# Attention and a gated two-layer product on one core: weight transfers issued by another engine, decoding moved, the last partial product reordered

## The chip, the cores and the metric

One Trainium2 chip, one of its cores. TensorE (PE) multiplies, VectorE (DVE), ScalarE (ACT) and GpSimd (POOL) work on elements, and SyncE (SP) issues transfers; ACT can issue transfers too. Each engine takes its instructions in the order in which the program lists them. The metric is the device time of one execution in microseconds (us), lower is better. The kernel before took 1116.28 us, the median of 1116.28, 1114.55 and 1116.56.

## The reference

```python
def _attn_ref(q, k, v):                    # 8 batches, 12 heads, S = 448, D = 64
    scale = 1.0 / np.sqrt(q.shape[-1])
    scores = scale * np.matmul(q, k.transpose(0, 1, 3, 2)) - np.log(S)
    attn = 1.0 / (1.0 + np.exp(-scores))
    return np.matmul(attn, v)
...
x = attn_out.transpose(0, 2, 1, 3).reshape(B * S, H * D)     # 3584 x 768
h = x @ w_in                                                 # 3584 x 2048
g = h * np.clip(h + 3.0, 0.0, 6.0) / 6.0
return g @ w_out                                             # 3584 x 768
```

`w_in` and `w_out` come as 8-byte floats and are turned into 4-byte ones on the chip.

## The kernel before

**Products.** Both large products run as a 2x2 block scheme with seven products instead of eight (P1, P5, P6, P2, P7, P3, P4 in the order of work). Each is done in three passes, from a high and a low part of both operands. A pair of batches is one step of the block scheme, so there are four pairs, n = 0 to 3.

**Stages.** The attention of four batches comes first, then the first product of pair 0, the attention of batch 4, the first product of pair 1, the attention of batches 5 and 6, the first product of pair 2, the attention of batch 7, and the first product of pair 3. The second product of all pairs ends the program. The first product of a pair is four quads (jj = 0 to 3); a quad is seven products for two row blocks, 14 units of 9 matmuls on one line, L305.

**Around one unit of the first product.** `load_w1` (L268) brings a weight tile "raw" (four buffers) from scratch memory. `split_w` makes its high part on ACT (L274) and the low part on VectorE (L275), in a tile "w". Between the products, `seed` on ACT (L313) copies the sum of P1 into the bank of P2 before P6 goes on adding to P1's bank. `keep` (L317) holds the sum of P5, `seed2` on VectorE (L321) makes the start of P3 before P7 goes on in P1's bank, and `h22` (L325) makes a last sum before P4. ACT and VectorE apply the gate (L335, L338), VectorE forms differences (L343), and SP stores the results in scratch memory "gd" (L346).

**Decoding.** `prep(which, j, ...)` decodes the 8-byte weights, w_in for which = 0 and w_out for which = 1, in eight parts j. Each part has two loads "st" (L108), two operations on ACT (L118), ten on VectorE (L123 to L133), two additions on POOL (L137) and four sums there (L146), and seven stores to scratch memory (L151), "wd1" for w_in and "wd2" for w_out. The tile of the decoded weights is "wa".

**Second product.** `load_g` (L391) and `load_w2` (L386) bring its operands "gr" and "w2", `split_2` splits them, and `unit` (L416) is nine matmuls, three passes for each of three output chunks. `keep`, `plus` and `out` (L425, L429, L443, L446) carry sums out. `open_two` closes the memory of the attention and opens that of the second product, from which the first "gr" and "w2" tiles come.

**What sets the order.** Every piece of work is put in a list with a place, `at(place, f, ...)`, a planned time in us. The list is sorted, and PE, ACT, VectorE and POOL take their instructions in that order. A transfer issued by SP is ordered by the framework's own scheduler from the same list. A transfer's end is signalled on one of eight semaphores, which all transfers of SP and ACT use in turn; a transfer is not issued before the previous one on its semaphore has landed.

The places of the first product are set by these lines (TU is the planned time of a unit, q that of a quad's half):

```python
at(place + (2 * s - 5.3) * TU, split_w1, n, jj, k)
at(place + (2 * s - 5.3) * TU - 12, load_w1, n, jj, k)
...
at(p + 1 * TU + e, seed, i)
at(p + 5 * TU + e, seed2, i)
```

Of the kernel before, what the change touches and what calls it, by code (L numbers as in the profile page):

```python
# [15 lines left out]
B, H, S, D = 8, 12, 448, 64  # L16
DM, DF = 768, 2048
P = 128
NC = S // P
NP = H // 2  # L20
HC = DM // P // 2
HF = DF // P // 2
W = HC * P
NT = B // 2
# [9 lines left out]
P1, P5, P6, P2, P7, P3, P4 = range(7)  # L34
# [5 lines left out]
TU = 9 * TM  # L40
# [3 lines left out]
def tile_kernel(ctx: ExitStack, tc: tile.TileContext, qk, vP, w8, outT):  # L44
    nc = tc.nc
# [6 lines left out]
    def at(place, f, *args):  # L52
        todo.append((place, len(todo), f, args))

    dram = ctx.enter_context(tc.tile_pool(name="dram", bufs=1, space=bass.MemoryType.DRAM))
    wd1 = [dram.tile([P, NW, 2, W], F32, name=f"wd1_{j}", tag=f"wd1_{j}") for j in range(HF // 2)]
# [33 lines left out]
    def pair_banks(name, i=None):  # L90
        if i is None:
            i = turn[0]
            turn[0] += 1
        return four["pool"].tile([P, 2, 512], F32, tag=f"sc{i % 2}", name=name)

    def bank(name, k):
        return ps.tile([P, 512], F32, tag=f"pv{k}", name=name)
# [149 lines left out]
    def t_ops(n, c, early, upper, both, late, gap):  # L247


        b11, b12, b21, b22 = ((2 * n, c), (2 * n + 1, c), (2 * n, c + HC), (2 * n + 1, c + HC))  # L250
        for (place, copy), k, q in zip(early, (P1, P2), (b11, b21)):
            at(place, put, n, k, c, q, copy)
        at(upper[0], minus, b11, b12, b11)
        at(upper[0] + gap / 2, put, n, P5, c, b11, upper[1])
        for i, part in enumerate((
            (minus, b11, b22, b11), (put, n, P6, c, b11), (minus, b12, b22, b12), (minus, b21, b21, b11), (put, n, P4, c, b21),
        )):
            at(both + gap * i, *part)
        for (place, copy), k, q in zip(late, (P7, P3), (b12, b22)):
            at(place, put, n, k, c, q, copy)  # L260
# [3 lines left out]
    ring, rawt = {}, {}  # L264

    def load_w1(n, jj, k):
        t = one.tile([P, 2, W], F32, tag="raw", name=f"raw_{n}_{jj}_{k}", bufs=4)
        nc.sync.dma_start(out=t, in_=wd1[jj][:, k])  # L268
        rawt[n, jj, k] = t

    def split_w(keys, src):
# [10 lines left out]
    passes = ((0, 0), (0, 1), (1, 0))  # L282
# [3 lines left out]
    def quads(n, jj, place):  # L286
# [62 lines left out]
        for s, k in enumerate(range(NW)):  # L349
            at(place + (2 * s - 5.3) * TU, split_w1, n, jj, k)  # L350
            at(place + (2 * s - 5.3) * TU - 12, load_w1, n, jj, k)
            for i in range(2):
                at(place + (2 * s + i) * TU, product, i, k)
# [20 lines left out]
    x2, w2, graw, two = {}, {}, {}, {}  # L374
# [28 lines left out]
    def block(n, place):  # L403
        z, sn = {}, {}

        def unit(k, u):
            if u == 0:
                if k in (P6, P7, P4):
                    z[k] = z[P1]
                else:  # L410
                    t = pair_banks(f"y_{n}_{k}", n + (k != P1))
                    z[k] = [t[:, 0], t[:, 1], bank(f"yb_{n}_{k}", 2 * (n % 2) + (k != P1))]
            w, x = ring.pop((n, k, u)), x2.pop((n, k, u))
            for e in range(HC):
                for i, (wu, xu) in enumerate(passes):
                    nc.tensor.matmul(  # L416
                        z[k][e][:, :S], w[:, wu, e * P : (e + 1) * P], x[:, xu],
                        start=u == 0 and i == 0 and k in (P1, P5, P2, P3), stop=u == HF - 1 and i == 2,
                        skip_group_check=True,
                    )  # L420

        def keep(k):
            for e in range(HC):
                t = two["b"].tile([P, S], F32, tag=f"sn{k}{e}", name=f"sn2_{n}_{k}_{e}")
                nc.scalar.mul(t, z[k][e][:, :S], sixth)  # L425
                sn[k, e] = t

        def plus(dst, k, e, s):
            nc.vector.scalar_tensor_tensor(  # L429
                out=dst, in0=z[k][e][:, :S], scalar=sixth, in1=sn[s, e], op0=ALU.mult, op1=ALU.add  # L430
            )

        def middle():
            for e in range(HC):
                t = two["b"].tile([P, S], F32, tag=f"c12{e}", name=f"c12_{n}_{e}")
                plus(t, P6, e, P5)
                sn["c12", e] = t

        def out(k, s, eh, th):
            for e in range(HC):  # L440
                o = two["b"].tile([P, S], F32, tag="o", name=f"o_{n}_{k}_{e}", bufs=4)
                if s is None:
                    nc.scalar.mul(o, z[k][e][:, :S], sixth)  # L443
                else:
                    plus(o, k, e, s)
                nc.sync.dma_start(out=outT[2 * n + th, e + eh * HC], in_=o)  # L446

        d = HF * TU
        for k in range(NW):
            at(place + k * d - 26, load_g, n, k)  # L450
            if n == 0:
                at(place + k * d - 24, load_w2, k)
            for u in range(HF):
                at(place + k * d + u * TU, unit, k, u)
                if u % 2 == 0:
                    at(place + k * d + u * TU - 6 * TU + 0.3, split_2, n, k, u)
        e = 0.3
        at(place + 1 * d + e, keep, P1)
        at(place + 2 * d + e, keep, P5)
        at(place + 3 * d + e, middle)  # L460
        at(place + 4 * d + e, out, P2, P1, 0, 0)
        at(place + 5 * d + e, out, P7, P5, 1, 1)
        at(place + 6 * d + e, out, P3, "c12", 0, 1)
        at(place + 7 * d + e, out, P4, None, 1, 0)

# [2 lines left out]
    marks, starts, taken = [], [], {}  # L470
# [28 lines left out]
    dve, act = nc.vector.tensor_copy, nc.scalar.copy  # L499
    for c in range(HC):  # L500
        for n in range(NT):
            own = [taken[2 * n + (h % 2), c + HC * (h // 2)] for h in range(4)]
            free = marks[n - 1] + HF * q if n else 0.0
            start = marks[n]
            if n == 0:
                early = ((own[0], dve), (own[2], dve))
                upper, both, gap = (max(own[1], own[0] + 1.2), dve), own[3] + 0.1, 1.4
                late = ((own[3] + 11, dve), (own[3] + 12.5, dve))
            elif n == 1:
                early = ((free - 11.6 * TU + 2.2 * c, act), (free - 0.5 + 9 * c, dve))  # L510
                upper, both, gap = (free - 9.6 * TU + 3 * c, act), free + 0.7 + 9 * c, 1.2
                late = ((start - 5 + 1.3 * c, dve), (start + 2 * TU + 1.5 * c, act))
            else:
                early = ((free - 11.6 * TU + 2.2 * c, act), (free - 5.6 * TU + 2.2 * c, act))
                upper, both, gap = (own[1] + 0.1, dve), own[3] + 0.1, 1.2 if n < 3 or c < 2 else 0.1
                if n == 2:
                    late = ((start - 30 + 10 * c, dve), (start - 25 + 10 * c, dve))
                else:
                    late = ((start + 4 * TU + 1.5 * c, act), (start + 6 * TU + 1.5 * c, act))
            t_ops(n, c, early, upper, both, late, gap)  # L520
    for j in range(HF):
        prep(0, j, (8, 26, 44, 74, 92, 110, 128, 146)[j], 9)
    for j, place in enumerate((
        marks[0] + 40, marks[1] + 18, marks[1] + 50, starts[2] + 26, starts[2] + 45, marks[2] + 14, marks[2] + 42, marks[2] + 68
    )):
        prep(1, j, place, 12)
    at(marks[3] + 6, open_two)
    at(now + 5.5, close_one)
    first = now
    at(now - 0.01, open_four, "psy")  # L530
    for n in range(NT):
        block(n, now)
        now += NW * HF * TU
# [52 lines left out]
```

## Time and profile before

| what | us |
|---|---|
| median of three runs | 1116.28 |
| the profiled execution's own time | 1117.07 |
| its span in the trace | 1115.2 |
| first attention, A0 | 3.74 to 136.34 |
| first product, pair 0, Z0 | 136.34 to 244.06 |
| attention of batch 4, A1 | 244.06 to 276.87 |
| first product, pair 1, Z1 | 276.87 to 383.24 |
| attention of batches 5 and 6, A2 | 383.24 to 449.63 |
| first product, pair 2, Z2 | 449.63 to 564.70 |
| attention of batch 7, A3 | 564.70 to 597.51 |
| first product, pair 3, Z3 | 597.51 to 703.28 |
| second product, Y | 703.28 to 1111.12 |

The stages are cut at the first matmul of each, from the timeline of TensorE, in microseconds from the start of the span. The span is that of the hardware's record of one execution; 1.87 us of the execution's own time lie outside it. The names A0 to Y are used below. "Idle before" in a timeline row stands in brackets at its end, with the engine and line that ended the idle time.

### The profile page before, as it was taken

How to read it: one execution, taken by the hardware profiler on the slowest of the kernel's cores; microseconds unless marked ns; L12 is line 12 of the kernel's file. 1: busy time of each engine (PE TensorE's matmuls, PEld its weight loads, DVE VectorE, ACT ScalarE, POOL GpSimd, SP SyncE). 2: the span in 40 equal slices, each digit the busy share in tenths (PEclk: the TensorE clock that was granted, in tenths of full speed). 3: DMA queues.
4: the chain of work that ended last, by engine and by line, in shares of the span. 5: the costliest groups of instructions: out<-in, count | busy, mean ns of one | idle time of the engine just before them, and what ended most of it. 6: DMA issues, size and time to landing. Idle time of an engine off the chain costs nothing.

```text
span 1115.2 us, 17907 instructions
## 1 busy us (share of the span) xinstructions
PE 1087.1 (97%) x6720; PEld 880.5 (79%) x6720; DVE 816.8 (73%) x1101; ACT 622.2 (56%) x841; POOL 149.1 (13%) x102
## 2 busy tenths in 40 slices
PE   8999998999999999999899999999999999999998
PEld 3447697974998743898756889999999999999997
DVE  4898799997699869799958577766655655665663
ACT  7878845457554678544467354554554455445542
POOL 1524533200033003233300000000000000000000
PEclk9999999999999999999899999999999999999999
DMA  7997998965598746899743984674533553454341
GB/s 248 294 327 231 332 336 277 338 243 169 167 318 294 278 135 211 299 309 316 243 163 99 379 301 162 263 332 157 199 132 133 182 182 132 134 173 175 110 143 60
DMA packets 95271, 250.23 MB, mean 224 GB/s; under 512 B 10576, under 2 KB 66256, under 8 KB 90704
## 3 DMA queue, kind: packets, MB, share of 16 engines
q1 hardware_dynamic: 95040, 249.01, 64.9%
q8 instruction: 53, 0.87, 0.3%
q14 instruction: 34, 0.28, 0.1%
q10 hardware_dynamic: 144, 0.07, 0.0%
HBM read 164.63 MB, written 84.41 MB: 223 GB/s over the span
## 4 chain that ended last, share of the span: by engine, by line
PE 73%; DVE 10%; DMA 8%; issue 5%; POOL 2%; ACT 2%; SPq 0%; ACTq 0%; DVEq 0%; POOLq 0%
PE y L416 24%; PE z L305 20%; PE yb L416 12%; PE sc L198 7%; PE pv L224 7%; DMA raw<-wd 2%; DVE w L275 2%; DMA gr<-gd 2%; POOL ws L146 1%; PE sc L193 1%; DVE t L343 1%; DMA st<-wi 1%; PE pv L218 1%; DVE g L338 1%; POOL wa L137 1%
## 5 line engine op out<-in xcount | busy, mean ns | idle before, releaser
L305 PE MATMUL z<-x,w 128*128 128x448 f32 x2016 | 420.5, 371 | 14.8 <-DVE z L321 12.8
L305 PEld LDWEIGHTS z<-x,w 128*128 128x128 f32 x2016 | 383.7, 191 | 52.9 <-issue 11.4
L416 PE MATMUL y<-x,w 128*128 128x448 f32 x1344 | 307.9, 364 | 0.0
L416 PEld LDWEIGHTS y<-x,w 128*128 128x128 f32 x1344 | 252.0, 187 | 19.9
L275 DVE TENSOR_TENSOR w<-w,w 128x768 fp32r<-128x768 f32 x112 | 107.3, 958 | 147.4 <-ACT w L274 146.3
L204 ACT ACTIVATE a<-sc,bias_s 128x896 f32<-128x896 f32 x168 | 168.4, 1009 | 52.4 <-PE sc L198 37.1
L274 ACT CAST w<-w 128x768 fp32r<-128x768 f32 x112 | 93.8, 838 | 184.6 <-PE yb L416 180.9
L416 PE MATMUL yb<-x,w 128*128 128x448 f32 x672 | 171.9, 364 | 0.0
L275 DVE TENSOR_TENSOR w<-raw,w 128x768 fp32r<-128x768 f32 x112 | 124.8, 1116 | 43.9 <-ACT w L274 40.2
L198 PE MATMUL sc<-qk 64*64 64x448 f32 x1152 | 149.5, 544 | 5.5 <-DMA qk<-qk 3.7
L224 PE MATMUL pv<-a,v 64*64 64x448 f32 x1152 | 149.6, 537 | 3.5 <-DVE xr L233 1.3
L416 PEld LDWEIGHTS yb<-x,w 128*128 128x128 f32 x672 | 126.0, 187 | 9.9
L399 DVE TENSOR_TENSOR x<-gr,x 128x896 fp32r<-128x896 f32 x112 | 121.6, 1086 | 6.5 <-ACT x L398 6.5
L137 POOL TENSOR_TENSOR wa<-wa,st 128x768 f32<-128x768 f32 x32 | 64.6, 2017 | 403.2 <-DVE st L133 328.7
L274 ACT CAST w<-raw 128x768 fp32r<-128x768 f32 x112 | 93.2, 832 | 38.3 <-PE z L305 17.0
L398 ACT CAST x<-gr 128x896 fp32r<-128x896 f32 x112 | 104.9, 937 | 6.5 <-DMA gr<-gd 6.5
L198 PEld LDWEIGHTS sc<-qk 64*64 64x64 f32 x1152 | 53.5, 134 | 66.0 <-issue 43.4
L224 PEld LDWEIGHTS pv<-a,v 64*64 64x64 f32 x1152 | 54.3, 133 | 61.7 <-issue 47.2
L335 ACT ACTIVATE g<-z,bias 128x448 f32<-128x448 f32 x96 | 59.8, 633 | 75.9 <-PE z L305 43.0
L335 ACT ACTIVATE g<-snh,bias 128x448 f32<-128x448 f32 x32 | 21.5, 671 | 78.1 <-DVE snh L325 75.1
L338 DVE SCALAR_TENSOR_TENSOR g<-g,z 128x448 f32<-128x448 f32 x96 | 58.4, 613 | 6.6 <-ACT g L335 6.6
L241 DVE TENSOR_TENSOR x<-xr,x 128x448 fp32r<-128x448 f32 x84 | 56.8, 678 | 8.5 <-ACT x L240 6.4
(43 smaller groups left out, 679.0 us busy)
## 6 DMA issues: line engine op xcount, KB each, us to landing
gr<-gd SPq DMA_DIRECT2D x28, 1792.0 KB, 8.2
raw<-wd SPq DMA_DIRECT2D x112, 384.0 KB, 4.8
gd<-t SPq DMA_DIRECT2D x128, 224.0 KB, 4.0
gd<-g SPq DMA_DIRECT2D x96, 224.0 KB, 3.9
qk<-qk SPq DMA_DIRECT2D x47, 448.0 KB, 5.7
st<-wi SPq DMA_DIRECT2D x16, 768.0 KB, 5.5
wd<-ws SPq DMA_DIRECT2D x64, 192.0 KB, 5.2
st<-wo SPq DMA_DIRECT2D x16, 768.0 KB, 5.6
```

The costliest lines, as they stand in the source:

```text
L137: nc.gpsimd.tensor_tensor(out=a, in0=a, in1=e, op=ALU.add)
L198: nc.tensor.matmul(sc[halves[h], j, :S], k[halves[j], ks], q[halves[j]], start=True, stop=True)
L204: nc.scalar.activation(a, sc[:, :, :S], AF.Sigmoid, bias=bias_s, scale=scale)
L224: nc.tensor.matmul(pv[b, hp][h][halves[j], :S], v[halves[h], j * NC + c], a[halves[h], j], start=c == 0 and not (second and shared), stop= ...
L274: nc.scalar.copy(h, src)
L275: nc.vector.tensor_tensor(out=l, in0=src, in1=h.bitcast(F32), op=ALU.subtract)
L305: nc.tensor.matmul(z[i, k][:, :S], w[:, wu, c * P : (c + 1) * P], X[n, k, c][:, xu], start=m == 0 and k in (P1, P5), stop=m == 3 * HC - 1, ...
L335: nc.scalar.activation(new(i, o), src(i, o), AF.Relu, bias=bias_3, scale=1.0)
L338: nc.vector.scalar_tensor_tensor(out=g[i, o], in0=g[i, o], scalar=6.0, in1=src(i, o), op0=ALU.min, op1=ALU.mult)
L398: nc.scalar.copy(x[:, 0], src)
L399: nc.vector.tensor_tensor(out=x[:, 1], in0=src, in1=x[:, 0].bitcast(F32), op=ALU.subtract)
L416: nc.tensor.matmul(z[k][e][:, :S], w[:, wu, e * P : (e + 1) * P], x[:, xu], start=u == 0 and i == 0 and k in (P1, P5, P2, P3), stop=u == H ...
```

## The change

It has four parts. The weight loads of the first product are issued by ACT instead of SP. `open_two` is placed 24 us later in the plan. The places of the decoding are moved: w_in's parts earlier, w_out's first part later, three instead of two of w_out's parts in the attention of batches 5 and 6, and two instead of three in the first product of pair 2; with it, the casts of pair 2's last operands go from VectorE in the attention to ACT at the start of the first product. The last product of the last pair, P4, runs as 24 matmuls for one output chunk after another, and each chunk is copied out when it is done.

```diff
     def load_w1(n, jj, k):
         t = one.tile([P, 2, W], F32, tag="raw", name=f"raw_{n}_{jj}_{k}", bufs=4)
-        nc.sync.dma_start(out=t, in_=wd1[jj][:, k])
+        nc.scalar.dma_start(out=t, in_=wd1[jj][:, k])
...
+        def column(k, e):
+            if e == 0:
+                z[k] = z[P1]
+            for u in range(HF):
+                w, x = ring[n, k, u], x2[n, k, u]
+                for i, (wu, xu) in enumerate(passes):
+                    nc.tensor.matmul(
+                        z[k][e][:, :S], w[:, wu, e * P : (e + 1) * P], x[:, xu],
+                        start=False, stop=u == HF - 1 and i == 2, skip_group_check=True,
+                    )
...
-        def out(k, s, eh, th):
-            for e in range(HC):
+        def out(k, s, eh, th, es=range(HC)):
+            for e in es:
...
             for u in range(HF):
-                at(place + k * d + u * TU, unit, k, u)
+                if (n, k) != (NT - 1, P4):
+                    at(place + k * d + u * TU, unit, k, u)
                 if u % 2 == 0:
-                    at(place + k * d + u * TU - 6 * TU + 0.3, split_2, n, k, u)
+                    at(place + k * d + u * TU - 6 * TU + 0.3 - (u == HF - 2), split_2, n, k, u)
...
-        at(place + 7 * d + e, out, P4, None, 1, 0)
+        if n < NT - 1:
+            at(place + 7 * d + e, out, P4, None, 1, 0)
+        else:
+            for h in range(HC):
+                at(place + (6 + h / HC) * d + 0.01, column, P4, h)
+                at(place + (6 + (h + 1) / HC) * d + e, out, P4, None, 1, 0, (h,))
...
-                if n == 2:
-                    late = ((start - 30 + 10 * c, dve), (start - 25 + 10 * c, dve))
-                else:
-                    late = ((start + 4 * TU + 1.5 * c, act), (start + 6 * TU + 1.5 * c, act))
+                late = ((start + 4 * TU + 1.5 * c, act), (start + 6 * TU + 1.5 * c, act))
...
-        prep(0, j, (8, 26, 44, 74, 92, 110, 128, 146)[j], 9)
+        prep(0, j, (7, 22, 38, 70, 87, 104, 121, 138)[j], 9)
...
-        marks[0] + 40, marks[1] + 18, marks[1] + 50, starts[2] + 26, starts[2] + 45, marks[2] + 14, marks[2] + 42, marks[2] + 68
+        marks[0] + 50, marks[1] + 18, marks[1] + 50, starts[2] + 2, starts[2] + 19, starts[2] + 43, marks[2] + 22, marks[2] + 56
...
-    at(marks[3] + 6, open_two)
+    at(marks[3] + 30, open_two)
```

On VectorE, in the first product of pair 2, the rows ahead of quad 3's first seed2 (L321) were these before. In a name such as w_2_6_4 stand the pair, the row block and the product; wa_1_7 and st_1_7_1 are the last decoded part of w_out.

```order
L343 TENSOR_TENSOR t4_2_2_1_5461<-g21_2_2_1_5449,t2_2_2_1_5429 128x448
L123 TENSOR_SCALAR wa_1_7_5324<-wa_1_7_5324 128x768
L125 TENSOR_SCALAR wa_1_7_5324<-wa_1_7_5324 128x768
L241 TENSOR_TENSOR x_3_0_0_5491<-xr_6_0_4386,x_3_0_0_5491 128x448
L275 TENSOR_TENSOR w_2_6_4_5494<-raw_2_3_4_5365,w_2_6_4_5494 128x768
L127 SCALAR_TENSOR_TENSOR wa_1_7_5324<-st_1_7_1_5363,wa_1_7_5324 128x768
L241 TENSOR_TENSOR x_3_0_1_5510<-xr_6_1_4513,x_3_0_1_5510 128x448
L131 TENSOR_SCALAR st_1_7_1_5363<-wa_1_7_5324 128x768
L133 SCALAR_TENSOR_TENSOR st_1_7_1_5363<-st_1_7_1_5363 128x768
L275 TENSOR_TENSOR w_2_6_5_5526<-raw_2_3_5_5405,w_2_6_5_5526 128x768
L241 TENSOR_TENSOR x_3_0_2_5529<-xr_6_2_4629,x_3_0_2_5529 128x448
L321 TENSOR_TENSOR z_2_3_5_0_5541<-z_2_3_0_0_5439,sne_2_3_0_5508 128x448
```

The same stretch of VectorE now:

```order
L343 TENSOR_TENSOR t4_2_2_1_5473<-g21_2_2_1_5456,t2_2_2_1_5436 128x448
L241 TENSOR_TENSOR x_3_0_0_5503<-xr_6_0_4415,x_3_0_0_5503 128x448
L275 TENSOR_TENSOR w_2_6_4_5506<-raw_2_3_4_5372,w_2_6_4_5506 128x768
L241 TENSOR_TENSOR x_3_0_1_5521<-xr_6_1_4538,x_3_0_1_5521 128x448
L275 TENSOR_TENSOR w_2_6_5_5539<-raw_2_3_5_5412,w_2_6_5_5539 128x768
L241 TENSOR_TENSOR x_3_0_2_5542<-xr_6_2_4643,x_3_0_2_5542 128x448
L321 TENSOR_TENSOR z_2_3_5_0_5554<-z_2_3_0_0_5446,sne_2_3_0_5519 128x448
```

The five operations of decoding that stood there (L123 to L133) are gone from the stretch, and the other rows keep their order.

Counted over the whole order of VectorE, the decoding operations between one quad's second seed2 and the next quad's first are these. Before quad 1 of pair 0 there were 9 of part 7 (a tenth came between the two seed2 of quad 0) and are now 5. Before quads 1, 2 and 3 of pair 2 there were 10, 10 and 10, and are now 6, 7 and 5 (with one more between the two seed2 of quad 1 and one between those of quad 2). In the attention of batches 5 and 6 there were 20 and are now 30. Around pair 1 nothing moves.

On ACT, in the first product of pair 3, the rows from the end of quad 0's gates to the seeds of quad 1 (L313) were these before:

```order
L335 ACTIVATE g12_3_0_1_6265<-z_3_0_5_1_6161,bias_3_107 128x448
L274 CAST w_3_2_2_6273<-raw_3_1_2_6163 128x768
L335 ACTIVATE g21_3_0_0_6288<-z_3_0_0_0_6041,bias_3_107 128x448
L335 ACTIVATE g21_3_0_1_6310<-z_3_0_0_1_6065,bias_3_107 128x448
L274 CAST w_3_2_3_6317<-raw_3_1_3_6197 128x768
L313 COPY z_3_1_3_0_6333<-z_3_1_0_0_6300 128x448
L313 COPY z_3_1_3_1_6347<-z_3_1_0_1_6323 128x448
```

The same stretch of ACT now, with the semaphores that a row waits for (DMAHW0 to 7 are those of transfers):

```order
L335 ACTIVATE g12_3_0_1_6261<-z_3_0_5_1_6157,bias_3_107 128x448 [waits PE_49]
L268 DMA raw_3_1_5_6263<-wd1_1_58 128x768 [waits DMAHW3_49,DVE_49]
L274 CAST w_3_2_2_6269<-raw_3_1_2_6159 128x768
L335 ACTIVATE g21_3_0_0_6284<-z_3_0_0_0_6041,bias_3_107 128x448 [waits PE_49]
L335 ACTIVATE g21_3_0_1_6306<-z_3_0_0_1_6065,bias_3_107 128x448 [waits DMAHW4_49,DVE_49,PE_49]
L268 DMA raw_3_1_6_6308<-wd1_1_58 128x768 [waits DMAHW2_49,Activation_49]
L274 CAST w_3_2_3_6313<-raw_3_1_3_6193 128x768 [waits DMAHW0_49]
L313 COPY z_3_1_3_0_6329<-z_3_1_0_0_6296 128x448 [waits PE_49]
L313 COPY z_3_1_3_1_6343<-z_3_1_0_1_6319 128x448 [waits PE_49]
```

The two loads, which stood on SP before, now stand on ACT ahead of the cast and the seeds.

On SP, at the same place in pair 3, the rows now are these. They start at the store of quad 0's first gate; "gr" and "w2" are the first operands of the second product.

```order
L346 DMA gd_3_0_89<-g11_3_0_0_6176 128x448 [waits DMAHW1_49,DVE_49]
L391 DMA gr_0_0_6780<-gd_0_0_68 128x3584 [waits DMAHW4_49,DMAHW3_49,DMAHW6_49,DMAHW2_49,PE_49]
L386 DMA w2_0_6807<-wd2_0_61 128x3072 [waits DMAHW3_49,Activation_49]
L346 DMA gd_3_0_89<-g11_3_0_1_6191 128x448 [waits DMAHW4_49,DVE_49]
L391 DMA gr_0_1_6898<-gd_0_1_69 128x3584 [waits DMAHW5_49]
L386 DMA w2_1_6921<-wd2_1_62 128x3072 [waits DMAHW6_49,Activation_49]
L346 DMA gd_3_5_94<-g22_3_0_0_6212 128x448 [waits DMAHW0_49,DVE_49]
L346 DMA gd_3_5_94<-g22_3_0_1_6228 128x448 [waits DMAHW1_49,DVE_49]
L346 DMA gd_3_1_90<-t1_3_0_0_6247 128x448 [waits DMAHW2_49,DVE_49]
```

The operands' transfers keep their place behind the first store, as before; the two weight loads that stood among these rows are gone. The holder of DMAHW3 ahead of raw_3_1_5 is the transfer of w2_0, and the holder of DMAHW2 ahead of raw_3_1_6 is the store of t1_3_0_0.

## The prediction

> **What bounds the kernel now.** I read the summary first, then the stages, then the pauses of TensorE.
>
> ```profile
> span 1115.2 us, 17907 instructions
> PE 1087.1 (97%) x6720; PEld 880.5 (79%) x6720; DVE 816.8 (73%) x1101; ACT 622.2 (56%) x841; POOL 149.1 (13%) x102
> ```
>
> TensorE is busy 97% of the span, and the change leaves every matmul in place. So time can only come from or go into its pauses, the slow-clock stretches behind them, and the two ends. I cut the span at the matmuls into the stages named above. The columns are: stretch, length, then busy time (and instructions) of PE, weight loads, DVE, ACT and POOL, the granted clock, the DMA share and GB/s.
>
> ```profile
> 3.74:136.34 132.60, 130.02 (x1344) 67.78 (x1344) 105.20 (x144) 104.91 (x123) 52.43 (x36) 1.00 0.86 290
> 136.34:244.06 107.72, 104.68 (x509) 95.67 (x505) 99.02 (x137) 53.15 (x84) 29.88 (x18) 0.98 0.87 302
> 276.87:383.24 106.37, 104.15 (x509) 95.78 (x505) 89.19 (x129) 53.37 (x86) 18.68 (x12) 0.98 0.78 260
> 449.63:564.70 115.07, 108.36 (x508) 97.86 (x505) 103.22 (x139) 53.64 (x85) 37.36 (x23) 0.96 0.84 284
> 597.51:703.28 105.77, 102.92 (x508) 94.55 (x505) 75.48 (x117) 53.60 (x85) 0.00 (x0) 1.00 0.70 247
> 703.28:1111.12 407.84, 407.84 (x2017) 377.75 (x2015) 245.67 (x278) 197.92 (x254) 0.00 (x0) 1.00 0.47 168
> ```
>
> The last row is the second product: 2016 matmuls in 407.84 us without a pause, 0.2023 each. A stage of the first product has 504, so it could take 102.0. The four (Z0 to Z3, rows two to five) are 5.7, 4.4, 13.1 and 3.8 above that: 27.0 us is all that better scheduling can win there. TensorE's timeline says where they lie (start, length, engine, line, operation; in brackets the pause before and what ended it):
>
> ```profile
> 174.94 3.51 PE L305 MATMUL z<-x,w 128*128 128x448 f32 x16 [1.20 <-DVE w L275]
> 180.30 2.23 PE L305 MATMUL z<-x,w 128*128 128x448 f32 x7 [1.84 <-DVE z L321]
> 345.03 2.20 PE L305 MATMUL z<-x,w 128*128 128x448 f32 x5 [2.22 <-DVE z L321]
> 518.96 1.34 PE L305 MATMUL z<-x,w 128*128 128x448 f32 x3 [1.97 <-DVE z L321]
> 551.01 2.21 PE L305 MATMUL z<-x,w 128*128 128x448 f32 x5 [4.72 <-DVE z L321]
> 640.01 7.53 PE L305 MATMUL z<-x,w 128*128 128x448 f32 x36 [2.10 <-DVE z L321]
> 648.29 2.06 PE L305 MATMUL z<-x,w 128*128 128x448 f32 x9 [0.75 <-DVE snh L325]
> ...
> 181.17:184.58 3.41, 3.41 (x11) 0.50 1.02 397
> 345.01:348.42 3.41, 3.39 (x9) 0.50 0.86 263
> 519.09:522.50 3.41, 3.41 (x10) 0.50 0.94 289
> 549.81:556.64 6.83, 5.63 (x15) 0.50 0.63 202
> ```
>
> All pauses end with VectorE, mostly with seed2 (L321), which P7 needs. The last four rows are stretches at half clock (length, PE busy, clock): 3.41 us behind a pause of about 2 us cost 1.7 of work each, and 5.63 busy behind the 4.72 cost 2.8. So Z0 lost 3.04+1.7 = 4.7, Z1 2.22+1.7 = 3.9, Z2 6.69+1.7+2.8 = 11.2, and Z3 2.85 without a slow stretch.
>
> **Decoding moved.** VectorE is late where decoding stands ahead of a seed2. The tile of the decoded weights alone, in Z0 and Z2 (same columns; VectorE's busy time is the first number after the length):
>
> ```profile
> 136.34:244.06 107.72, 14.44 (x20) 4.54 (x5) 29.88 (x18) 0.98 0.87 302
> 449.63:564.70 115.07, 17.91 (x24) 5.40 (x6) 37.36 (x23) 0.96 0.84 284
> ...
> 340.87 3.47 DVE L275 TENSOR_TENSOR w<-raw,w 128x768 fp32r<-128x768 f32 x2
> 341.03 2.50 POOL L137 TENSOR_TENSOR wa<-wa,st 128x768 f32<-128x768 f32 x1 [16.17 <-DMA raw<-wd]
> 346.26 0.94 DVE L275 TENSOR_TENSOR w<-raw,w 128x768 fp32r<-128x768 f32 x1
> ```
>
> An operation of decoding takes 0.72 to 0.75 (14.44/20, 17.91/24), and the same subtraction 0.94 alone against 1.74 beside POOL, so each decode costs its ten operations, about 7.3 us, and some slowing by POOL besides. In Z2 the order of the changed program has two decodes in place of three. Between the last seed2 of quad 2 and the first of quad 3 it has 5 such operations instead of 10. Those directly ahead of quad 3's seed2 are gone. That is 5×0.73 = 3.7, plus one POOL addition less beside the subtractions (0.8), 4.5 against a pause of 4.72. In quad 2 the pause is 1.97, and 8 operations are left of 10 (1.5 less). Both pauses nearly go, and with them their slow stretches: of 11.2 I take 10.5. If the relief were only half as good, the pauses would be 2.5 and 1.2. In Z0 the last part of decode 7 comes earlier, so 5 operations instead of 10 precede quad 1's seed2: 3.7 against pauses of 3.04, so 4.7 goes. What is late next there is the seed, below. The third decode goes to the attention before Z2, in the room that six casts leave on VectorE. ACT now makes those at the start of Z2; each is smaller than a weight cast (0.83, row below), so together they stay under 5 us of a stage in which ACT is busy 53.64 of 115: 0. Z1's decoding is unmoved, so its 3.9 stay.
>
> **Weight loads on ACT.** 112 loads leave SP's queue. Before, SP waited where a raw buffer was not free:
>
> ```profile
> SPq L268 <- DVE w L275: 125.1, 72, 12.2
> ...
> 0.87 0.37 ACTq L171 DMA_DIRECT2D qk<-qk  x1
> ```
>
> 125.1 us of waiting in 72 cases cost TensorE nothing. Issuing costs about 0.37, so 28 loads cost ACT 10 us of a stage in which it is busy 53 of 106. That is covered. What isn't covered is order: ACT now stops at each load until its buffer is free and until the earlier DMA on the same semaphore has landed (eight semaphores go round all DMAs of SP and ACT), and behind the load stand the cast L274 and the seed L313. How much room has a seed? The plain case and the worst:
>
> ```profile
> 451.83 0.52 ACT L313 COPY z<-z 128x448 f32<-128x448 f32 x1 [0.82 <-PE z L305]
> 453.48 0.38 SPq L108 DMA_DIRECT2D st<-wo  x1
> st<-wo SPq DMA_DIRECT2D x1, 768.0 KB, 6.4
> ...
> 612.85 0.45 SPq L386 DMA_DIRECT2D w<-wd  x1
> 614.79 1.46 SPq L268 DMA_DIRECT2D raw<-wd  x1
> 626.43 5.16 SPq L346 DMA_DIRECT2D gd<-t  x3
> w<-wd SPq DMA_DIRECT2D x1, 1536.0 KB, 13.5
> raw<-wd SPq DMA_DIRECT2D x1, 384.0 KB, 17.4
> gd<-t SPq DMA_DIRECT2D x1, 224.0 KB, 12.2
> ...
> 628.31 0.96 ACT L313 COPY z<-z 128x448 f32<-128x448 f32 x2
> 632.24 0.83 ACT L274 CAST w<-raw 128x768 fp32r<-128x768 f32 x1 [2.97 <-DMA raw<-wd]
> ```
>
> P6 is due 36 matmuls after a quad begins. In Z2's first quad that is 449.63+7.3 = 456.9, and the first seed is ready at 452.35: 4.6 of room. A load there waits for a decode's load like the 6.4 one. I take 0.5 for it (0 to 3), 1.5 for the first loads of Z0, which stand among the sigmoids of the attention with 2.6 us of idle TensorE in all (0 to 3), and 1.2 in Z1 (0 to 2.2, as its pause).
>
> In Z3 the burst of the second product's first operands (1.5 MB and more apiece, from 612) fills the queue. A 224 KB store of t1, issued at 626.43, lands 12.2 later, at 638.6. In the changed order the load raw_3_1_6 waits on the semaphore which that store holds, and raw_3_1_5 before it on that of the 1.5 MB transfer (612.85+13.5 = 626.4). Behind raw_3_1_6 stand a cast (0.83) and the seeds of quad 1. Before, the first seed ended at 628.8, and P6 was due at 597.51+162×0.2023 = 630.3. Now it ends at 638.6+0.83+0.54 = 640.0, so TensorE stops for 9.7. The old 2.85 falls inside that. A pause this long has no row; the nearest is 4.72 with 2.8 of slow clock (none after 640.01, so 0 to 2.8); I take 2.8. Z3: 9.7−2.85+2.8 = **+9.65**, between −2.85 (ACT isn't held) and +9.65.
>
> The Trainium skill, "TensorE: Matmul & The Clock Gate", Part 1, "The HAM clock gate", says that the clock halves after an idle window of about 3.4 us and comes back after a busy one. By it the term is 1.7, not 2.8, and the sum 1.1 lower; the 3.41 rows agree in length, but they follow pauses of about 2 us, shorter than a whole window, so the rows decide.
>
> **The second product opened later.** The first transfers of that product still stand behind the store of quad 0's first gate in SP's order, as before: 0. If they came later, the burst would move and Z3's cost with it (the rival "no hold").
>
> **Last product by chunk.** The matmuls are the same. Its operands must be ready before the first chunk ends, and their splitting is placed one unit earlier.
>
> ```profile
> 1110.55 0.98 ACT L443 ACTIVATE o<-y 128x448 f32<-128x448 f32 x2 [12.28 <-PE y L416]
> 1111.42 0.55 ACT L443 ACTIVATE o<-yb 128x448 f32<-128x448 f32 x1
> outT<-o SPq DMA_DIRECT2D x1, 224.0 KB, 2.1
> ```
>
> Two of the three copies and their stores (2.1 each) now lie behind matmuls. The last copy alone starts some 0.2 sooner, and its store has no other ahead: −0.4 (−1.0 to +0.5).
>
> **Sum.** Z0 −4.7, Z2 −10.5, Z1 +1.2, the attentions +2.0, Z3 +9.65, end −0.4: −2.75. The profiled execution took 1117.07 (span 1115.2 and 1.87 around it), so 1114.3. It lies 0.8 above the median 1116.28, which gives **1113.5**.
>
> **Rivals.**
> - *No hold in Z3* (chance 0.22). The store lands sooner because two weight loads are no longer ahead of it on SP's queue, or the burst comes later; then Z3 is −2.85 and the whole 1113.5−9.65−2.85 = 1101.0. For it: a raw tile took 17.4 only since it stood behind the burst. Against it: the store itself still stands there. The Trainium skill, "DMA: Bandwidth & Descriptors", "Issuing engines are not separate DMA queues", says that issuing from another engine saves only the sequencer's time; by it the 2.85 would stay and the case give 1103.9. No load of weights from ACT is in this trace.
> - *ACT's order costs in every stage* (0.2, slower). Each load that holds ACT for longer than a seed's room, 4.6 in the plain case and 1.5 in Z3's quad 1 (630.3−628.8), stops TensorE. Three more quads with a pause like the 2.10 row are 6.3: 1119.8. For it: SP's longest wait for a raw buffer was 12.2. Against it: most are early waits, for ACT comes to the load later than SP did.
> - *The decoding doesn't relieve VectorE* (0.11, slower). POOL's slowing moves along, and Z2's quad 3 keeps 4.72+2.8 = 7.5: 1121.0.
>
> **How the numbers follow.** My forecast has 0.47, with a range of its own of 1109 to 1117.5 (Z3's slow clock, the attentions, half of the relief). All cases together reach from 1101 to 1121. About 0.2%, 2.2 us, is what a measurement here can tell from no change, so the borders are 1114.05 and 1118.5. Faster: 0.28 of my case and the 0.22 without a hold, 0.50. Same: 0.17 of mine and 0.05 of the slower two, 0.22. Slower: 0.28.
>
> **What would show it.** Right: no pause before seed2 in Z0 and in Z2's quads 2 and 3; in Z3 one pause of 9 to 10 us near 630 ended by the seed L313, with ACT at its load's wait since 628. Wrong: a Z3 of 103 us, ACT idle behind loads ahead of other seeds, or VectorE still last before P7 in Z2.

## The result and the profile after

The changed kernel took 1146.07 us, the median of four runs (1141.71 to 1146.95), beside 1116.42 for the kernel before (1114.55 to 1117.36). The ratio is 1.026, with a 95% interval from 1.0231 to 1.0289: 2.6% slower, where 0.25% faster was forecast. The profiled execution took 1146.95, with a span of 1145.1.

These are the stages of the kernel after, cut at the first matmul of each as before (columns: stretch, length, busy time and instructions of PE, weight loads, DVE, ACT and POOL, clock, DMA share, GB/s). The rows are A0, Z0, Z1, A2, Z2, Z3 and Y.

```profile
3.69:147.66 143.97, 133.51 (x1345) 64.41 (x1345) 113.11 (x148) 105.91 (x124) 53.68 (x37) 0.99 0.82 276
147.66:256.25 108.59, 106.39 (x508) 95.68 (x505) 94.83 (x133) 52.76 (x83) 27.68 (x17) 0.98 0.80 274
289.00:399.08 110.08, 105.90 (x509) 95.40 (x505) 88.31 (x129) 53.71 (x86) 18.68 (x12) 0.98 0.71 236
399.08:477.08 78.00, 69.70 (x673) 27.55 (x672) 60.09 (x82) 53.42 (x63) 25.39 (x17) 0.94 0.72 249
477.08:586.22 109.14, 106.45 (x509) 96.19 (x505) 90.39 (x130) 55.05 (x89) 20.08 (x14) 0.98 0.72 237
618.97:733.73 114.76, 106.50 (x508) 96.99 (x505) 76.44 (x117) 54.30 (x85) 0.00 (x0) 0.96 0.65 228
733.73:1141.58 407.85, 407.85 (x2017) 377.75 (x2015) 245.27 (x277) 198.69 (x254) 0.00 (x0) 1.00 0.48 169
```

A2 of the kernel before was this:

```profile
383.24:449.63 66.39, 64.72 (x674) 25.97 (x673) 53.43 (x83) 52.12 (x61) 10.39 (x7) 1.00 0.62 200
```

Against before, A0 is 11.4 us longer, A2 11.6, Z3 9.0, Z1 3.7 and Z0 0.9; Z2 is 5.9 shorter. The second product is the same, and the end behind its last matmul shrank from 4.1 to 3.5. The two attentions hold 23 us of a net loss of 30. In A0 TensorE was idle for 2.6 us before and is now for 10.5 (143.97−133.51); in A2 it was 1.7 and is 8.3. A2's busy time grew as well, from 64.72 to 69.70 at a mean clock of 0.94: at three pauses of 2.3 to 2.7 us the clock is halved, for 8.5 us of busy time in all, and half of that, 4.3, is lost.

The list of waits of the kernel after says who it waits for (waiter, what it waited for, us in total, times, longest):

```profile
PE z L305 <- ACT z L313: 15.7, 7, 8.3
...
PE sc L193 <- ACT a L204: 7.9, 4, 2.6
...
PE sc L198 <- ACT a L204: 4.9, 7, 1.8
...
PE pv L224 <- ACT a L204: 3.6, 4, 2.7
...
PE z L305 <- DVE z L321: 1.3, 1, 1.3
```

VectorE's seed2, 12.8 us before, is down to 1.3. ACT's seed (L313), which wasn't in this list before, has 15.7, and ACT's sigmoids (L204) have 16.4 (2.9 before). So TensorE now waits for ACT where it waited for VectorE. The longest wait is the one of Z3. ACT's timeline there, then the row of TensorE and the clock (stretch, length, PE busy, clock):

```profile
641.16 0.64 ACT L335 ACTIVATE g<-z,bias 128x448 f32<-128x448 f32 x1 [0.36 <-PE z L305]
646.95 0.33 ACTq L268 DMA_DIRECT2D raw<-wd  x1
647.31 0.83 ACT L274 CAST w<-raw 128x768 fp32r<-128x768 f32 x1 [5.52 <-DMA w<-wd]
648.05 0.63 ACT L335 ACTIVATE g<-z,bias 128x448 f32<-128x448 f32 x1
649.76 0.64 ACT L335 ACTIVATE g<-z,bias 128x448 f32<-128x448 f32 x1 [1.08 <-issue]
658.65 0.33 ACTq L268 DMA_DIRECT2D raw<-wd  x1
659.02 0.83 ACT L274 CAST w<-raw 128x768 fp32r<-128x768 f32 x1 [8.62 <-DMA gd<-t]
659.75 0.95 ACT L313 COPY z<-z 128x448 f32<-128x448 f32 x2
...
660.33 7.84 PE L305 MATMUL z<-x,w 128*128 128x448 f32 x24 [8.26 <-ACT z L313]
...
656.00:666.24 10.24, 5.91 (x16) 0.50 1.01 366
```

ACT comes to the load raw_3_1_5 at 641.8 and issues it at 646.95; the transfer of w2_0, the earlier holder of its semaphore, landed at 646.87. It comes to raw_3_1_6 at 650.4 and issues it at 658.65; the store of t1, the earlier holder, landed at 658.57. Each load goes out 0.08 us behind the landing. Then come the cast, the seed, and TensorE, which had stood for 8.26, and lost 2.95 more (half of 5.91) to the slow clock. This is the stop that was forecast.

Loads also hold ACT where the prediction took 1.5 and 0.5 us. In A0 a load stands between two sigmoids, and in Z2's first quad one stands ahead of the first seed:

```profile
132.07 1.91 ACT L204 ACTIVATE a<-sc,bias_s 128x896 f32<-128x896 f32 x2
136.80 0.33 ACTq L268 DMA_DIRECT2D raw<-wd  x1
137.23 1.01 ACT L204 ACTIVATE a<-sc,bias_s 128x896 f32<-128x896 f32 x1 [3.25 <-DMA wd<-ws]
...
480.88 0.33 ACTq L268 DMA_DIRECT2D raw<-wd  x1
481.25 0.83 ACT L274 CAST w<-raw 128x768 fp32r<-128x768 f32 x1 [3.50 <-DMA st<-wo]
481.99 0.53 ACT L313 COPY z<-z 128x448 f32<-128x448 f32 x1
```

For 3.25 us, until a store of decoded weights had landed, no sigmoid ran, and TensorE stopped for 1.91 at 138.29. In Z2, 3.50 us went by until a load of coded weights had landed; there the seed's room held, and TensorE has no pause before 537.91. Two loads in A2 held sigmoids in the same way, and TensorE stopped for 2.58 and 2.69. Setting the issue of each of the 112 loads against the last thing it waited for, ACT stood before 41 of them for more than 0.45 us, 75 us in all: 43 us (17 loads) for another transfer on its semaphore, 32 us (24 loads) for VectorE to free the raw buffer. What reached TensorE from the seeds came mostly from the first kind: of the seven pauses that ended with a seed, six (13.5 of the 15.7 us) follow a load that had stood for a transfer, and one (2.2) a load that had stood 0.99 for VectorE.

### The profile page after: what moved, and what is told of

The parts are those of the page before. It is cut to its first block, busy times and chain, and to the rows that moved or that the text cites. A ratio compares the mean times of both kernels' runs of the same rounds, so it can differ in the third digit from the quotient of the medians.

```text
span 1145.1 us, 17763 instructions
## 1 busy us (share of the span) xinstructions
PE 1100.7 (96%) x6720; PEld 879.1 (77%) x6720; DVE 814.6 (71%) x1095; ACT 627.1 (55%) x847; POOL 145.8 (13%) x102
## 4 chain that ended last, share of the span: by engine, by line
PE 67%; DVE 10%; DMA 9%; issue 7%; ACT 4%; POOL 3%; SPq 1%; ACTq 0%; DVEq 0%; POOLq 0%
PE y L416 23%; PE z L305 22%; PE yb L416 11%; PE sc L198 4%; PE pv L224 4%; DVE w L275 2%; DMA raw<-wd 2%; DVE g L338 2%; ACT w L274 2%; POOL ws L146 2%; DMA gd<-t 2%; DVE t L343 2%; POOL wa L137 1%; DMA v<-vP 1%; ACT a L204 1%
## 5 line engine op out<-in xcount | busy, mean ns | idle before, releaser
L305 PE MATMUL z<-x,w 128*128 128x448 f32 x2016 | 425.6, 373 | 17.3 <-ACT z L313 15.7
L305 PEld LDWEIGHTS z<-x,w 128*128 128x128 f32 x2016 | 384.1, 191 | 60.9 <-ACT z L313 18.4
L416 PE MATMUL y<-x,w 128*128 128x448 f32 x1296 | 297.0, 364 | 0.0
L416 PEld LDWEIGHTS y<-x,w 128*128 128x128 f32 x1296 | 243.0, 187 | 19.2
L275 DVE TENSOR_TENSOR w<-w,w 128x768 fp32r<-128x768 f32 x112 | 107.2, 957 | 147.7 <-ACT w L274 146.6
L204 ACT ACTIVATE a<-sc,bias_s 128x896 f32<-128x896 f32 x168 | 168.3, 1012 | 59.8 <-PE sc L198 39.3
L416 PE MATMUL yb<-x,w 128*128 128x448 f32 x648 | 166.1, 364 | 0.0
L275 DVE TENSOR_TENSOR w<-raw,w 128x768 fp32r<-128x768 f32 x112 | 116.4, 1040 | 69.2 <-ACT w L274 68.0
L224 PE MATMUL pv<-a,v 64*64 64x448 f32 x1152 | 152.0, 551 | 6.3 <-ACT a L204 3.6
L416 PEld LDWEIGHTS yb<-x,w 128*128 128x128 f32 x648 | 121.5, 187 | 9.5
L241 DVE TENSOR_TENSOR x<-xr,x 128x448 fp32r<-128x448 f32 x84 | 61.7, 737 | 9.8 <-ACT x L240 7.9
L233 DVE TENSOR_TENSOR xr<-pv,xr 128x448 f32<-128x448 f32 x48 | 29.8, 621 | 35.9 <-ACT xr L232 35.9
```

Of the source, the lines that this page charges most:

```text
L204: nc.scalar.activation(a, sc[:, :, :S], AF.Sigmoid, bias=bias_s, scale=scale)
L224: nc.tensor.matmul(pv[b, hp][h][halves[j], :S], v[halves[h], j * NC + c], a[halves[h], j], start=c == 0 and not (second and shared), stop= ...
L241: nc.vector.tensor_tensor(out=x[:, 1], in0=xr[q], in1=x[:, 0].bitcast(F32), op=ALU.subtract)
L275: nc.vector.tensor_tensor(out=l, in0=src, in1=h.bitcast(F32), op=ALU.subtract)
L305: nc.tensor.matmul(z[i, k][:, :S], w[:, wu, c * P : (c + 1) * P], X[n, k, c][:, xu], start=m == 0 and k in (P1, P5), stop=m == 3 * HC - 1, ...
L416: nc.tensor.matmul(z[k][e][:, :S], w[:, wu, e * P : (e + 1) * P], x[:, xu], start=u == 0 and i == 0 and k in (P1, P5, P2, P3), stop=u == H ...
```

## The experiments

**Which part costs.** Four kernels took the change apart. The theory (S): ACT stops at its loads and holds what stands behind them. The rival (D): it is the denser decoding.

The change with its loads back on SP:

```diff
-        nc.scalar.dma_start(out=t, in_=wd1[jj][:, k])
+        nc.sync.dma_start(out=t, in_=wd1[jj][:, k])
```

> The changed kernel with its weight loads issued by SP again; the rest of the change stays. Theory S (ACT stops at its loads and holds the sigmoids of the attention and the seeds): the first attention is back near 133 us and that of batches 5 and 6 near 67, the fourth stage of the first product near 106; the whole is 1102 to 1108, below the kernel before, since the moved decoding still relieves the third stage (115.1 to about 105). Rival D (the denser decoding costs the attentions): the two attentions stay near 144 and 78 us and the whole is 1125 or more.

The kernel before with that one line changed the other way:

> The kernel before with its weight loads issued by ACT and nothing else. Theory S: it is slower by 20 us or more, 1136 to 1150, with the first attention 6 us or more longer than its 132.6, and a pause near 8 us ended by a seed in the fourth stage of the first product. Rival D: within 10 us of before (only that last pause), with attentions of 133 and 66 us.

The kernel before with the places of the decoding and the late casts of the change:

```diff
-        prep(0, j, (8, 26, 44, 74, 92, 110, 128, 146)[j], 9)
+        prep(0, j, (7, 22, 38, 70, 87, 104, 121, 138)[j], 9)
...
-        marks[0] + 40, marks[1] + 18, marks[1] + 50, starts[2] + 26, starts[2] + 45, marks[2] + 14, marks[2] + 42, marks[2] + 68
+        marks[0] + 50, marks[1] + 18, marks[1] + 50, starts[2] + 2, starts[2] + 19, starts[2] + 43, marks[2] + 22, marks[2] + 56
...
-                if n == 2:
-                    late = ((start - 30 + 10 * c, dve), (start - 25 + 10 * c, dve))
-                else:
-                    late = ((start + 4 * TU + 1.5 * c, act), (start + 6 * TU + 1.5 * c, act))
+                late = ((start + 4 * TU + 1.5 * c, act), (start + 6 * TU + 1.5 * c, act))
```

> The kernel before with all places of the decoding (w_in's and w_out's parts, and the late casts of the third pair) moved as in the change and nothing else. Theory S: 1102 to 1108, with the third stage of the first product near 105 us. Rival D: 1120 or more, with attentions near 144 and 78 us.

The kernel before with `column` and the later `open_two`:

> The kernel before with the last partial product by output chunk and the second product's memory opened later, and nothing else. Both theories: the end behind the last matmul is 3.5 us in place of 4.1, the stages are as before, so 0.4 to 0.6 us less, which the comparison can hardly tell from no change. If opening later moves the first transfers of the second product, the fourth stage of the first product loses its 2.9 us of pauses.

The stages of their profiled executions, and the medians with the ratio to before:

| us | before | after | sp_loads | act_only | decode_only | column_open |
|---|---|---|---|---|---|---|
| A0 | 132.6 | 144.0 | 141.4 | 140.9 | 143.4 | 132.8 |
| Z0 | 107.7 | 108.6 | 104.3 | 111.1 | 103.8 | 107.7 |
| Z1 | 106.4 | 110.1 | 106.4 | 108.5 | 106.3 | 106.3 |
| A2 | 66.4 | 78.0 | 70.5 | 72.7 | 70.5 | 66.4 |
| Z2 | 115.1 | 109.1 | 106.8 | 121.7 | 106.6 | 115.2 |
| Z3 | 105.8 | 114.8 | 104.9 | 113.2 | 106.0 | 105.5 |
| median | 1116.2 | 1146.1 | 1117.7 | 1150.5 | 1119.3 | 1116.1 |
| ratio (95%) | | 1.026 (1.0231 to 1.0289) | 1.0007 (0.9995 to 1.002) | 1.03 (1.0276 to 1.0324) | 1.0029 (1.0009 to 1.0048) | 0.9997 (0.9987 to 1.0007) |

Neither theory stands alone. The kernels sp_loads and decode_only fall between the two forecasts, and act_only is 0.5 us above the range of S. The loads on ACT cost 34 us by themselves and 28 on top of the rest, so S names the larger part. The two parts overlap: in A0 the loads alone cost 8.3, and 2.6 on top of the moved decoding. But D is right about A0 and part of A2: the moved decoding wins 3.4 to 4.0 us in Z0 and 8.3 to 8.5 in Z2, as forecast from VectorE's rows, and gives it back in the attentions, 8.8 to 10.8 in A0 and 4.1 in A2. Opening later did nothing that shows. The column shortens the end behind the last matmul by 0.5 in the trace, which the medians can't tell from no change.

Why the decoding costs in A0 and A2, in the kernel sp_loads, where no load stands on ACT. First its A0 and A2 as windows, then ACT in A0, then VectorE, POOL and TensorE in A2:

```profile
3.80:145.21 141.41, 132.69 (x1344) 56.50 (x1345) 115.04 (x148) 105.62 (x124) 54.98 (x37) 1.00 0.82 278
...
388.75:459.27 70.52, 65.29 (x673) 28.36 (x672) 60.99 (x82) 53.33 (x63) 22.24 (x15) 1.00 0.73 246
```

```profile
49.58 1.01 ACT L204 ACTIVATE a<-sc,bias_s 128x896 f32<-128x896 f32 x1 [0.75 <-PE sc L198]
53.23 0.91 ACT L118 ACTIVATE wa<-st 128x768 f32<-128x768 f32 x1 [2.64 <-DMA st<-wi]
```

```profile
420.58 2.16 DVE L241 TENSOR_TENSOR x<-xr,x 128x448 fp32r<-128x448 f32 x1
422.67 2.75 DVE L245 TENSOR_TENSOR xr<-xr,xr 128x448 f32<-128x448 f32 x2
...
425.88 0.63 DVE L241 TENSOR_TENSOR x<-xr,x 128x448 fp32r<-128x448 f32 x1
426.42 0.62 DVE L233 TENSOR_TENSOR xr<-pv,xr 128x448 f32<-128x448 f32 x1
...
420.33 1.94 POOL L137 TENSOR_TENSOR wa<-wa,st 128x768 f32<-128x768 f32 x1 [3.30 <-DVE st L133]
...
427.10 0.60 PE L224 MATMUL pv<-a,v 64*64 64x448 f32 x3 [2.33 <-DVE xr L233]
```

In A0 the first operation of a decode stands on ACT ahead of sigmoids and waits for its load. That load went out at 45.2, when POOL had freed its buffer, and landed at 53.2; ACT stands idle for 2.64 us ahead of the next sigmoid. Such waits of the decodes' heads for transfers make 9.4 us in A0, against 1.4 before, and TensorE's waits for sigmoids there grow from 1.1 to 6.2. That is 5.1 of the 8.8; the rest is not followed here. In A2 the third decode puts POOL beside VectorE: a subtraction (L241) that takes 0.63 alone takes 2.16, the sum of the attention's two halves (L233) comes late, and TensorE waits 2.33. A second wait of this kind, at 439.86, is 2.01.

**Is it the sigmoids that are held?** The changed kernel with quad 0's loads, the ones issued in an attention, back on SP.

```diff
-        nc.scalar.dma_start(out=t, in_=wd1[jj][:, k])
+        (nc.sync if jj == 0 else nc.scalar).dma_start(out=t, in_=wd1[jj][:, k])
```

> The changed kernel with the weight loads of quad 0 of each pair, which are the ones issued during an attention, back on SP; those of quads 1 to 3 stay on ACT. Theory S (loads on ACT stop the sigmoids): the attentions come down to those of the kernel with all loads on SP, 141.4 and 70.5 us (from 144.0 and 78.0), and the stages of the first product stay as in the changed kernel (108.6, 110.1, 109.1, 114.8): 1135 to 1138. Rival Q (transfers on a second queue crowd out the attention's own): the attentions fall by half of that at most, 1141 or more.

It took 1136.26 us (ratio 1.0188, 1.0174 to 1.0202), with A0 and A2 back at the lengths of the kernel with all loads on SP:

```profile
3.74:145.35 141.61, 133.86 (x1345) 56.59 (x1345) 114.80 (x148) 105.62 (x124) 54.69 (x37) 0.99 0.83 279
397.57:467.82 70.25, 67.00 (x674) 28.75 (x673) 60.95 (x82) 53.38 (x63) 22.23 (x15) 0.98 0.74 247
```

The other stages stay within 1.2 us, at 109.6, 109.8, 108.0 and 114.0. So 10 us of the loads' 28 arise in the attentions, and the rest in the first product, where 18.5 us of pauses ended by a seed stay in this kernel. The edit takes the transfers off ACT's queue too, so by itself it can't rule out rival Q; that ACT stood still ahead of the late sigmoids is seen in the rows of the changed kernel above.

**Does ACT come to its loads too early?** The changed kernel with each load 5 us ahead of its cast instead of 12.

```diff
-            at(place + (2 * s - 5.3) * TU - 12, load_w1, n, jj, k)
+            at(place + (2 * s - 5.3) * TU - 5, load_w1, n, jj, k)
```

> The changed kernel with each weight load placed 5 us ahead of its cast in the plan instead of 12, still on ACT. Theory E (ACT is stopped because it reaches a load before its buffer and its semaphore are free, not by issuing it): most of the stops go, the pause ended by a seed in the fourth stage of the first product is under 3 us, and the whole is 1118 to 1130. Rival L (the load's own flight is what the casts need in advance): the casts L274 wait for their tiles instead, and the whole is 1140 or more.

Theory E fell: 1142.8 us (1.0249, 1.0227 to 1.0272). The waits for VectorE are gone from the loads (none over 0.45 us, from 32 us), but those for semaphores stay, 39 us of 43. ACT's timeline in Z3 again:

```profile
648.66 0.63 ACT L335 ACTIVATE g<-z,bias 128x448 f32<-128x448 f32 x1
659.24 0.33 ACTq L268 DMA_DIRECT2D raw<-wd  x1
659.84 0.64 ACT L335 ACTIVATE g<-z,bias 128x448 f32<-128x448 f32 x1 [10.55 <-DMA gd<-g]
```

The load is raw_3_1_4 now, and its semaphore's holder is the transfer of w2_1, which landed at 659.16. The gate behind it waited in addition for a store, issued behind the same burst, that landed at 659.73; the row names this later one, which would have stopped ACT without the load too. Coming later traded one holder for another in this place. Both signs of rival L came: the casts wait for their tiles in flight (37 us in 24 cases, in the list of waits), and the whole is over 1140. TensorE's pauses ended by a seed fell from 15.7 to 9.3 us, 7.65 of them in Z3, but those ended by seed2 rose from 1.3 to 8.6. So this run can't price the buffers alone; that the semaphores' stops are what reached TensorE rests on the changed kernel's trace.

**Is the pause in Z3 the burst's?** The changed kernel with the first four operand transfers of the second product issued by ACT at their places, late in Z3.

```diff
-        nc.sync.dma_start(out=t, in_=wd2[k])
+        (nc.scalar if k < 2 else nc.sync).dma_start(out=t, in_=wd2[k])
...
-        nc.sync.dma_start(out=t, in_=gd[n][k])
+        (nc.scalar if n == 0 and k < 2 else nc.sync).dma_start(out=t, in_=gd[n][k])
```

> The changed kernel with the first four transfers of the second product's operands (2 gr, 2 w2) issued by ACT at their planned places, in the last quads of the fourth stage, in place of the start of that stage. If the pause of 8.3 us there comes from the burst of these transfers ahead of a store whose semaphore a load waits for, that stage falls from 114.8 to 104 to 107 us and the whole to 1136 to 1139. If the pause has another cause, the stage stays at 112 or more.

Z3 fell to 107.2, 0.2 above the expected range, and at quad 1 TensorE runs through. A pause of 3.12 ended by a seed appears at 709.75: that seed stands on ACT behind the transfer of w2_0, which went out at 708.81 when a store had landed. The whole is 1141.98 (1.0232, 1.0218 to 1.0246), 3 us over the expected range. In the profiled executions, Z3 won 7.6, and Z2, the end and A0 lost 1.3, 0.9 and 0.6, which is not followed here. The early burst, ahead of the store, is the cause of the 8.26.

**What is worth keeping.** The change without the loads on ACT and without w_in's new places:

```diff
-        nc.scalar.dma_start(out=t, in_=wd1[jj][:, k])
+        nc.sync.dma_start(out=t, in_=wd1[jj][:, k])
...
-        prep(0, j, (7, 22, 38, 70, 87, 104, 121, 138)[j], 9)
+        prep(0, j, (8, 26, 44, 74, 92, 110, 128, 146)[j], 9)
```

> The change without the weight loads on ACT and without the new places of w_in's decoding: w_out's places, the late casts, the last product by chunk. If the first attention's 8.8 us more (141.4 against 132.6) come from w_in's places, it is back at 133, with 70.5 for the attention of batches 5 and 6 and 106.6 for the third stage: 1110 to 1113, faster than before. If they come from elsewhere, the first attention stays near 141 and the whole near 1118.

It took 1112.55 us (0.9973, 0.9963 to 0.9984), and A0 is back:

```profile
3.82:136.22 132.40, 130.31 (x1344) 68.54 (x1344) 105.46 (x144) 105.04 (x123) 52.51 (x36) 1.00 0.86 290
```

So the 8.8 us there are w_in's places. In the next kernel w_out's last part moved into the attention of batch 7. Two more add to it the late burst (a3_burst), or w_in's last two parts a little earlier, at 127 and 143 in place of 128 and 146 (a3_j7):

```diff
-        marks[0] + 50, marks[1] + 18, marks[1] + 50, starts[2] + 2, starts[2] + 19, starts[2] + 43, marks[2] + 22, marks[2] + 56
+        marks[0] + 50, marks[1] + 18, marks[1] + 50, starts[2] + 26, starts[2] + 45, marks[2] + 22, marks[2] + 56, starts[3] + 2
```

> The kernel w_out_column with two parts of w_out decoded in the attention of batches 5 and 6 at their old places, and the last part in the attention of batch 7, where VectorE is busy 20 of 33 us. If the 3.8 us more of batches 5 and 6 (70.2 against 66.4) come from the third part there, that stage is back at 66.4, the attention of batch 7 grows by less than 1.5 us, and the whole is 1108 to 1110. If they come from the moved casts or from anything else, the stage stays near 70 and the whole at 1112 or more.

> The kernel a3_decode with the first four operand transfers of the second product issued by ACT at their planned places, late in the fourth stage. If the early burst is what makes that stage's weight tiles late where SP issues them (pauses of 0.5 and 1.3 us left), the stage falls from 105.9 to 103 to 104 and the whole is 1106 to 1108. If ACT is stopped there as it was at 709 us in the kernel act_burst_late (3.1 us), nothing is won: within 1 us of a3_decode or slower.

> The kernel a3_decode with the last two parts of w_in planned 1 and 3 us earlier. If VectorE's decoding ahead of quad 1's seed2 is all that delays it, the first stage loses up to 2.5 us of its pauses (0.7 and 1.9): 105 to 107 in place of 107.6. If the heads of decoding then wait for their loads ahead of the sigmoids, as in the kernel with all of w_in's places moved, the first attention grows by 1 to 3 us and nothing is won.

The kernel a3_decode took 1109.63 us (0.9936, 0.9921 to 0.9951), within the 1108 to 1110 expected. A2 is 64.7: against 70.2 in w_out_column, the third part cost 5.6 there, and against 66.4 before, the casts that left A2 win 1.7. The attention of batch 7 is unchanged at 32.8, but Z3 grew from 105.9 to 109.0. With the late burst of act_burst_late's edit, a3_burst took 1105.07 us (0.9901, 0.9885 to 0.9917), a little below the 1106 to 1108 expected and 1.0% below the kernel before. The rows are Z3 of a3_decode with its pause, and Z3 of a3_burst:

```profile
588.23:697.27 109.04, 105.23 (x508) 95.97 (x505) 78.66 (x122) 53.50 (x85) 0.00 (x0) 0.98 0.70 245
...
632.44 2.01 PE L305 MATMUL z<-x,w 128*128 128x448 f32 x5 [3.81 <-DVE z L321]
```

```profile
588.58:691.34 102.76, 102.51 (x508) 94.78 (x505) 77.62 (x121) 53.52 (x85) 0.00 (x0) 1.00 0.76 256
```

102.76 is the 102.0 of 504 matmuls without a stop and 0.76. In a3_decode two raw tiles that SP issued beside the burst land 17.4 and 18.4 us after their issue, and seed2 waits for what is made of the second. The edit a3_j7 won nothing (1110.83, 0.9953, 0.9936 to 0.9971). Its Z0 is 108.8, where quad 1 now waits 2.14 for a subtraction (L275) in place of seed2, and its A0 is 132.9, 0.5 longer; so neither expectation held.

## Why the prediction was wrong

The forecast was 1113.5, with a range of 1101 to 1121 over all cases; the time was 32.6 above the forecast. Of the signs named beforehand both kinds came: seed2 is quiet in Z0 and Z2 and Z3 has its one long pause, and ACT stands behind loads ahead of other seeds. What failed above all are the terms of the attentions. Point by point:

- **Decoding on VectorE, Z0 −4.7 and Z2 −10.5**: right in mechanism, and too large. With the loads on SP it is −3.4 and −8.3, 11.7 together for 15.2; a wait of 1.8 for a subtraction and one of 1.0 for seed2 stay in quad 3 of Z2.
- **"The third decode goes to the attention before Z2, in the room that six casts leave on VectorE"**: failed. A2 grows by 4.1 us, the 5.6 of the third part less what the casts leave, for POOL slows VectorE there where TensorE waits for the attention's sums. The busy share of VectorE said nothing of it.
- **w_in's places**: the forecast counted what they remove ahead of quad 1 and gave their cost in A0 as nothing, without a row. It is 8.8 us: with mostly 15 to 17 us planned between parts in place of 18, the head of a decode comes to ACT before its load has landed. This is the first failed step: a cost put at nothing.
- **"I take 0.5 for it (0 to 3), 1.5 for the first loads of Z0"**: failed, the second step. On top of the moved decoding, the loads on ACT cost 2.6 in A0 and 7.5 in A2 (8.3 and 6.3 without it). The 0.5 was worked out from a seed's room in Z2's first quad, and there nothing was lost; that the same quad's loads stand among the sigmoids of A2 had no term. The bound of 3 came from TensorE's idle time in A0 before the change (2.6 us), and that is no bound on what a new wait can add. The bound to be taken was the time in flight of the transfer waited for, once for each load that stands between sigmoids: 4.5 to 8.9 us for the loads of w_in's parts in the kernel before, and 5.1 to 7.0 for the four transfers that held a load in A0 and A2 after. Of A2's 7.5, 4.4 is TensorE's busy time, most of it the halved clock behind the new pauses, which the term left out too.
- **Z1 +1.2, none for Z0 and Z2's seeds**: mis-sized. The loads cost 3.7 in Z1, 4.3 in Z0 and 2.4 in Z2 (after against sp_loads). The slower rival had the mechanism, "ACT's order costs in every stage", and priced it at three pauses of 2.1; there were seven waits for a seed and fifteen for a sigmoid (none and eight before).
- **Z3 +9.65**: right, 9.0, with the place, the two semaphores and the engine as foretold. The pause was 8.26 for 9.7, and the slow clock cost 2.95 for 2.8. The estimate by the clock rule of the Trainium skill ("TensorE: Matmul & The Clock Gate", Part 1, "The HAM clock gate") was 1.7; the trace does not agree with it, for the slow stretch here was 10.24 us long, three times 3.41, and began within the pause.
- **Opened later 0, last product −0.4**: right; the end is 0.5 us shorter.

In the sum the forecast's gains on VectorE were 15.2 and the real ones 11.7; its costs in the attentions were 2.0 and the real ones 23.0. The attentions' 21.0, the 6.7 for the loads in Z0 and Z2, the 3.5 of smaller gains and 2.5 more in Z1 are 33.7. With 0.7 less in Z3 and at the end this accounts for the 32.6 to within half a microsecond.

## What to carry to other kernels

A transfer that is issued by an engine with work of its own is a wait put into that engine's work: price it by the flight of the slowest transfer it can meet on its semaphore, at every instruction behind it that a busy engine needs. Small slack of the busiest engine before a change does not bound what a wait costs after it. Where a loosely placed burst delays small loads on one queue, moving the burst later and to the other queue (6.3 us of Z3 here, 4.6 of the whole) did what moving the loads could not.

## What the runs showed of the hardware

A 384 KB tile issued by ACT during the burst landed in 6.8 to 9.4 us, against 16.7 to 17.1 for tiles issued by SP behind the same burst in the kernel sp_loads. These rows (transfer, issuing engine, size, us from issue to landing) are one tile on ACT and a 1.5 MB transfer of the burst, w2_1, in the kernel after, and one tile on SP in sp_loads:

```profile
raw<-wd ACTq DMA_DIRECT2D x1, 384.0 KB, 8.9
w<-wd SPq DMA_DIRECT2D x1, 1536.0 KB, 20.7
...
raw<-wd SPq DMA_DIRECT2D x1, 384.0 KB, 16.7
```

The tile on ACT went out at 636.84 and landed at 645.70, while w2_1, issued by SP at 636.17, landed at 656.88: a second queue is served beside the first. The Trainium skill, "DMA: Bandwidth & Descriptors", "Issuing engines are not separate DMA queues", holds that only the sequencer's time is saved. For a small transfer behind large ones these runs differ, in line with the section "Queues, rings and completion order" of that page of the Trainium skill, by which the engines take packets from the queues in turn.

The halved clock does not follow from a pause's length alone. In A2 of the kernel after, a pause of 2.33 us that ended at 437.16 was followed by 3.41 us at clock 0.50; in A2 of sp_loads a pause of 2.33 at the same piece of work was followed by none.
